# Four more chunks transposed by transfers instead of TensorE, in a retention layer followed by a Mish feed-forward

## The chip, the cores and the metric

The kernel runs on one core of one Trainium2 chip. A core has five engines that run their own instruction streams and meet at semaphores: TensorE (PE in the profile; its weight loads are listed as PEld), VectorE (DVE), ScalarE (ACT), GpSimd (POOL) and SyncE (SP). SP and POOL also issue the transfers (DMAs), which 16 DMA engines carry out. The metric is the time of one execution on the device, in microseconds, median of several runs. Before the change it is 296.61 us (three runs, 296.42 to 296.66).

## The reference

The inputs are q, k and v of shape (8 batches, 8 heads, 576 positions, 64), and two matrices, `w_in` (512 x 2048) and `w_out` (2048 x 512). The first part is causal attention without a softmax, with a decay per head; the second is a feed-forward layer with Mish on 4608 tokens of width 512.

```python
scores = scale * np.matmul(q, k.transpose(0, 1, 3, 2))
gamma = 1.0 - 2.0 ** (-5.0 - np.arange(H, dtype=np.float32))
Dmat = np.where(rel >= 0, gamma[:, None, None] ** rel[None, :, :], 0.0)   # rel = query - key position
attn = np.matmul(scores * Dmat, v)
x = attn.transpose(0, 2, 1, 3).reshape(B * S, H * D)
h = x @ w_in
g = h * np.tanh(softplus(h))
out = g @ w_out
```

## The kernel before

The decay is split into a factor on q, one on k and one on v by position, so that the attention becomes a linear recurrence: each batch is cut into chunks of 128 positions (four whole ones and a last one of 64, two such halves sharing one chunk), there are products inside a chunk, and a state of 64 x 64 per head is carried from chunk to chunk. In total there are 36 chunks. Chunks 0 to 7 are the first ones of the eight batches and are worked off by separate code at the start. From chunk 8 (`N0`) on every chunk goes through the same steps:

- `load(n)` (L298): three transfers issued by POOL bring q, k and v as float32. `vraw` has seven buffers, q and k (`qkraw`) have five. `paced` (L292) makes each load of chunks 12 and 13 wait until the sixth load before it has landed.
- `step_p(n)`, called P (L322): two VectorE instructions multiply q and k with their factors and write `qks` in bf16 (four buffers).
- `step_v(n)`, called V (L333): one instruction scales v into `vs`; on VectorE for n under 20, on POOL after that.
- `step_t(n)`, called T (L342): q and k are needed with the head dimension on the partitions. For n under `NT` (14) TensorE transposes `qks` in eight pieces (L351) into a PSUM bank, and ScalarE copies them to `qkT` (in two halves for chunks 8 to 11, L354 and L355, the second of which is put off by `flush`; in one copy for 12 and 13, L357). From chunk 14 on SP issues one transposing transfer from `qks` to `qkT` (L359). SP issues these in order with the stores of the output.
- `states` (L409) multiplies k with v for two chunks, and `sum_up` (L444) adds the products to the running state on VectorE (`total`, L452 to L464); a cast to `ssb` (L467) follows later.
- `step_s` (L364) forms the scores inside two chunks from `qkT`, `step_m` (L377) masks them on VectorE (`sm`).
- `visit(n)` (L524) belongs to chunks n and n + 1: it puts the state products of the next two chunks, the output products of these two (from `sm`, `vs`, `ssb` and `qkT`) and the scores of the next two on TensorE, and copies the result to `xT`, the input of the feed-forward part.
- `hold(n)` (L520) lets POOL copy one element of `qkT` of chunk n. As POOL works in order, its later loads are not issued until the transfer of that chunk has landed.

The feed-forward part works on tiles of four chunks. `g1(t, f)` makes one of 16 slices of the hidden layer of tile t (four matmuls of 128 x 512, then Mish on ScalarE), `g2(t, i)` a quarter of the 16 matmuls of a row block of the output. `product` (L551) issues one such matmul; while the counter `halved` is over 0, a matmul that is neither the first nor the last of its sum is issued as two of half the width.

The order of all work is written out by hand and fixed for each engine. The change lies in the loop over `u` from 0 to 23 (L753): its first 16 steps make the hidden layer of tile 1, the last 8 the first half of its output. Between them, dictionaries say at which `u` the steps of chunks 8 to 15 are put in (`ps` for P, `vs` for V, `ts_` for T). The visit of chunks 8 and 9 is at `u` = 17, that of 10 and 11 at `u` = 22; the states of chunks 8 and 9 are formed at `u` = 10, their cast to `ssb` is at `u` = 13. Loads of chunks 12, 13, 14, 15 and 16 are issued at `u` = 4, 8, 12, 16 and 20. The loop behind it (L800), over tiles 2 and up, is the same before and after.

Of the kernel before, what the change touches and what calls it, by code (L numbers as in the profile page):

```python
# [9 lines left out]
F32 = mybir.dt.float32  # L10
BF16 = mybir.dt.bfloat16
# [5 lines left out]
def kernel(  # L17
# [18 lines left out]
    nc = tc.nc  # L36
    B, H, S, D = q.shape
# [9 lines left out]
    NT = 14  # L47
# [242 lines left out]
    issued = []  # L290

    def paced(ins, n):  # L292

        if N0 + 3 < n < N0 + 6:
            behind(ins, issued[-6])
        issued.append(ins)

    def load(n, gate=None):  # L298
# [4 lines left out]
        vr = io.tile([P, H, D], F32, name="vraw", bufs=7)  # L303
        live[n] = {"qkr": qkr, "v": vr}
        for t, src in ((qkr[:, 0], q), (qkr[:, 1], k), (vr, v)):
            if c < 4:
                ins = nc.gpsimd.dma_start(  # L307
                    out=t, in_=src[b, :, ds(P * c, P), :].rearrange("h p d -> p h d"))
                paced(ins, n)
# [12 lines left out]
    def step_p(n):  # L322
        c = chunks[n][1]
        qks = io.tile([P, 2, H, D], BF16, name="qks", bufs=4)
        live[n]["qks"] = qks
        slots = qks.rearrange("p i (g x y) d -> p (i g) y x d", x=2, y=2)
        heads = live[n]["qkr"].rearrange("p i (g y x) d -> p (i g) y x d", x=2, y=2)
        factors = gqk[:, c].rearrange("p i (g y x) -> p (i g) y x", x=2, y=2)
        for y in range(2):
            nc.vector.tensor_tensor(slots[:, :, y], heads[:, :, y],  # L330
                                    factors[:, :, y].unsqueeze(3).to_broadcast([P, NP, 2, D]), op=OP.mult)
# [10 lines left out]
    def step_t(n, gate=None):  # L342
        flat = live[n]["qks"].rearrange("p i h d -> p (i h d)")
        qk = tr.tile([P, 2, NP, P], BF16, name="qkT", bufs=6)
        if n < NT:
            if n in (N0 + 2, N0 + 4):
                tp = ps_st.tile([P, 2 * NP, P], BF16, name="st")
            else:
                tp = ps_sc.tile([P, 4 * NP, P], BF16, name="sc")[:, 0:2 * NP]
            for i in range(2 * NP):  # L350
                nc.tensor.transpose(tp[:, i, :], flat[:, ts(i, P)], ident)  # L351
            if n < N0 + NCH:

                nc.scalar.copy(qk[:, 0], tp[:, 0:NP])  # L354
                later.append(lambda: nc.scalar.copy(qk[:, 1], tp[:, NP:2 * NP]))  # L355
            else:
                nc.scalar.copy(qk.rearrange("p i n t -> p (i n) t"), tp)  # L357
# [392 lines left out]
    ps = {0: 0, 4: 1, 8: 2, 11: 3, 18: 5, 21: 6, 23: 7}  # L750
    vs = {0: 0, 5: 1, 9: 2, 13: 3, 18: 4, 19: 5}
    ts_ = {3: 0, 7: 1, 12: 2, 14: 3, 19: 4, 21: 5}
    for u in range(24):  # L753
        j, w = divmod(u, 4)
        halved[0] = 2 if 0 < u < 5 else 0
        if u in ps:
            att(N0 + ps[u], "P")
        if u == 11:
            step_m(N0)
        if u in vs:  # L760
            att(N0 + vs[u], "V")
# [13 lines left out]
        elif u == 16:  # L775
            att(N0 + 4, "P")
# [3 lines left out]
        elif u == 22:  # L780
            visit(N0 + 2, ((ps_h, "hp"), (ps_h, "hp")), (act, dve))
            att(N0 + 6, "T")
# [6 lines left out]
        if u in ts_:  # L789
            att(N0 + ts_[u], "T")  # L790
# [107 lines left out]
```

## Time and profile before

| What | Value |
|---|---|
| Time, median of 3 runs | 296.61 us (296.42 to 296.66) |
| Profiled execution | 297.28 us, of which the span is 295.6 us |
| TensorE busy | 286.1 us, 97% of the span |
| VectorE, ScalarE, GpSimd busy | 140.0, 128.1, 124.9 us |
| Granted TensorE clock | 1.0 over the whole span |
| Transposing transfers | 22, median 2.8 us from issue to landing |
| Transposes of chunks by TensorE (L351) | 48 instructions, six chunks |
| Data moved by DMA | 47.45 MB, mean 161 GB/s |

Times in the views are counted from the start of the span. A line of a timeline gives the start, the duration, the engine, the line of the kernel, the operation, what it writes and reads, and how often; in square brackets it gives the idle time of the engine before it and what ended that. Matmuls overlap in their pipeline: one of 128 x 512 is listed with 0.38 us, but one starts every 0.216 us. A line of the windows gives, after the length of the window, the busy time and number of instructions of PE, PEld, DVE, ACT and POOL, then the granted clock, the share of the 16 DMA engines' time that packets took, and GB/s. Packets that take turns on an engine can add up to a share of over 1. A line of waits gives total us, how often, and the longest. In the DMA view q0 is the queue of the transfers that POOL issues and q1 that of SP; a line gives packets, MB and the share of the 16 engines' time. The loop over `u` begins at 48 us; the visit of chunks 8 and 9 begins at 65.8, that of 10 and 11 at 72.7; the loop over tiles 2 and up begins at 75.6.

### The profile page before, as it was taken

What the parts mean: (1) busy time and instruction counts of PE and PEld (TensorE: products, weight loads), DVE (VectorE), ACT (ScalarE), POOL (GpSimd) and SP (SyncE); (2) the same over time, 40 slices, a digit from 0 to 9 for tenths busy, and PEclk for the clock granted to TensorE, in tenths of its full rate; (3) what the DMA queues carried; (4) which work ended last, traced back from release to release, by engine and by line L of the source; (5) the groups of instructions that cost most, each with busy time, mean ns of one, the idle gap of its engine ahead of it and who ended that gap; (6) DMA issues with size and microseconds to landing.
All of it is one profiled execution on the core that took longest, in us unless ns stands there. A gap on an engine that the chain in (4) does not pass through costs nothing.

```text
span 295.6 us, 7898 instructions
## 1 busy us (share of the span) xinstructions
PE 286.1 (97%) x3447; PEld 159.7 (54%) x3486; DVE 140.0 (47%) x252; ACT 128.1 (43%) x210; POOL 124.9 (42%) x163
## 2 busy tenths in 40 slices
PE   7899999999999999999999999999999999999995
PEld 4666887556567454447645454545454544444443
DVE  5861549399954829454655454535453221000011
ACT  3856226776545534443443434343435333333200
POOL 8944678880167195855483636392020000000000
PEclk9999999999999999999999999999999999999999
DMA  7999999982498889799476837374222111011121
GB/s 154 234 204 204 205 328 337 336 237 85 109 270 190 168 229 254 232 145 330 116 204 164 260 90 237 108 229 115 68 71 71 38 38 65 9 35 49 59 71 71
DMA packets 44067, 47.45 MB, mean 161 GB/s; under 512 B 25984, under 2 KB 33152, under 8 KB 44032
## 3 DMA queue, kind: packets, MB, share of 16 engines
q0 software_dynamic: 15120, 31.20, 41.6%
q1 hardware_dynamic: 28768, 15.54, 20.7%
q8 instruction: 27, 0.44, 0.6%
q10 hardware_dynamic: 144, 0.20, 0.2%
q14 instruction: 8, 0.07, 0.1%
HBM read 37.75 MB, written 9.44 MB: 160 GB/s over the span
## 4 chain that ended last, share of the span: by engine, by line
PE 93%; DMA 2%; issue 1%; ACT 1%; POOL 1%; DVE 0%; POOLq 0%
PE hp L553 41%; PE ops L553 30%; PE hp L558 6%; PE ops L558 4%; DMA gT<-in_q_dram 2%; PE sc L373 1%; PE sc L428 1%; PE hp L504 1%; PE hp L487 1%; PE hp L634 1%; PE st L558 1%; POOL gT L107 1%; PE st L428 1%; PE sc L351 1%; PE sc L200 1%
## 5 line engine op out<-in xcount | busy, mean ns | idle before, releaser
L553 PE MATMUL hp<-xT,w_in_t 128*128 128x512 bf16 (+1 forms) x505 | 125.9, 376 | 0.9
L590 ACT ACTIVATE gT<-hp 128x512 bf16<-128x512 f32 x142 | 84.8, 598 | 95.3 <-PE hp L553 88.8
L553 PE MATMUL ops<-w_out_t,gT 128*128 128x512 bf16 x403 | 99.9, 379 | 2.0 <-issue 1.9
L553 PEld LDWEIGHTS <-w_in_t 128*128 128x128 bf16 x527 | 51.4, 98 | 53.9 <-issue 0.4
L553 PEld LDWEIGHTS <-gT 128*128 128x128 bf16 x470 | 44.7, 98 | 51.3
L642 DVE COPY res<-ops 128x512 f32<-128x512 f32 x28 | 19.3, 690 | 85.3 <-PE ops L553 85.2
L330 DVE TENSOR_TENSOR qks<-qkraw,gqk 128x512 bf16<-128x512 f32 x56 | 36.9, 709 | 0.0
L307 POOL DMA_DIRECT2D qkraw<-in_q_dram x24 | 21.5, 898 | 23.5 <-ACT gT L590 15.0
L337 POOL TENSOR_TENSOR vs<-vraw,gv 128x512 bf16<-128x512 f32 x16 | 16.8, 1068 | 25.0 <-PE hp L487 25.0
L516 DVE CAST xT<-hp 128x512 bf16<-128x512 f32 x13 | 9.0, 691 | 30.8 <-PE hp L504 30.8
L307 POOL DMA_DIRECT2D vraw<-in_v_dram x24 | 21.8, 907 | 1.8 <-DMA vraw<-in_v_dram 1.0
L307 POOL DMA_DIRECT2D qkraw<-in_k_dram x24 | 21.3, 886 | 1.0 <-DMA vpair<-in_v_dram 0.7
L516 ACT CAST xT<-hp 128x512 bf16<-128x512 f32 x14 | 8.2, 586 | 28.5 <-PE hp L504 28.5
L558 PEld LDWEIGHTS <-gT 128*128 128x128 bf16 x180 | 17.3, 98 | 3.7
L464 DVE TENSOR_TENSOR total<-sc,total 128x256 f32<-128x256 f32 x40 | 16.9, 422 | 1.0
L379 DVE TENSOR_TENSOR sm<-sc,mask 128x1024 bf16<-128x1024 f32 x14 | 17.0, 1214 | 0.6 <-PE sc L373 0.6
L558 PE MATMUL hp<-xT,w_in_t 128*128 128x256 bf16 x104 | 15.9, 272 | 0.0
L558 PEld LDWEIGHTS <-w_in_t 128*128 128x128 bf16 x106 | 10.4, 98 | 6.6 <-issue 0.2
L522 POOL COPY held<-qkT 128x1 bf16<-128x1 bf16 x8 | 1.5, 189 | 27.8 <-DMA qkT<-qks 27.8
L467 ACT CAST ssb<-total 128x768 bf16<-128x768 f32 (+3 forms) x13 | 11.6, 895 | 3.2 <-DVE total L464 3.2
L558 PE MATMUL ops<-w_out_t,gT 128*128 128x256 bf16 x96 | 12.4, 273 | 0.2
L553 PE MATMUL hp<-w_out_t,gT 128*128 128x512 bf16 x49 | 12.0, 379 | 0.2 <-issue 0.2
(132 smaller groups left out, 243.3 us busy)
## 6 DMA issues: line engine op xcount, KB each, us to landing
out_dram<-res SPq DMA_DIRECT2D x31, 256.0 KB, 2.4
qkraw<-in_q_dram POOLq DMA_DIRECT2D x24, 256.0 KB, 4.4
qkraw<-in_k_dram POOLq DMA_DIRECT2D x24, 256.0 KB, 4.5
vraw<-in_v_dram POOLq DMA_DIRECT2D x24, 256.0 KB, 4.7
w_out_t<-in_moe_w_out_dram POOLq DMA_DIRECT2D x4, 512.0 KB, 12.3
gT<-in_k_dram POOLq DMA_DIRECT2D x8, 128.0 KB, 7.1
gT<-in_v_dram POOLq DMA_DIRECT2D x2, 512.0 KB, 6.6
w_in_t<-in_moe_w_in_dram POOLq DMA_DIRECT2D x2, 512.0 KB, 10.3
```

Of the source, the lines that this page charges most:

```text
L307: ins = nc.gpsimd.dma_start(out=t, in_=src[b, :, ds(P * c, P), :].rearrange("h p d -> p h d"))
L330: nc.vector.tensor_tensor(slots[:, :, y], heads[:, :, y], factors[:, :, y].unsqueeze(3).to_broadcast([P, NP, 2, D]), op=OP.mult)
L337: engine.tensor_tensor(vs, live[n]["v"], gv[:, c, :].unsqueeze(2).to_broadcast([P, H, D]), op=OP.mult)
L379: nc.vector.tensor_tensor(sm.rearrange("p e x n i -> p (e x n) i"), live[n]["sc"].rearrange("p e x n i -> p (e x n) i"), mask.unsqueeze(1) ...
L428: ins = nc.tensor.matmul(to, lhsT=ks, rhs=vs, start=(x is not None or j == 0 and p == 0), stop=True, skip_group_check=True)
L464: nc.vector.tensor_tensor(new[:, k], st[:, j, x], total[b], op=OP.add)
L467: casts.append(lambda copy: copy(lows[:, 0:k], new[:, 0:k]))
L516: copy(xts[t][:, :, ds(P * s, 2 * P)].rearrange("p h (x j i) -> p j h x i", x=2, j=2)[:, j], both[j])
L553: newest[0] = nc.tensor.matmul(to, lhsT=w, rhs=x, start=first, stop=last)
L558: nc.tensor.matmul(to[:, ts(j, n)], lhsT=w, rhs=x[:, ts(j, n)], start=False, stop=False, skip_group_check=True)
L590: done = nc.scalar.activation(gts[t][:, f, :], hp, AX.Mish)
L642: copy(ot, ops)
```

## The change

Chunks 10 to 13 are no longer transposed by TensorE and copied by ScalarE: `NT` falls from 14 to 10, so SP issues four more transposing transfers, at `u` = 8, 9, 10 and 11 for chunks 10, 11, 12 and 13, and the one of chunk 14 moves to `u` = 18. On VectorE, P of 11 and 12 and V of 11 come before the sums of the states (`u` = 9), P of 13 follows those sums, P of 14 comes at `u` = 14. `paced` is gone. At `u` = 13 POOL holds for chunk 13's transfer, so the loads of chunk 15 and up are issued after it has landed. `qks` gets a fifth buffer, `vraw` loses its seventh. `halved` splits 29 more products, in `u` = 12 to 21; with the 32 transposes gone, the number of TensorE's instructions, weight loads among them, falls by six only.

```diff
-    NT = 14
+    NT = 10
...
-    issued = []
-    def paced(ins, n):
-        if N0 + 3 < n < N0 + 6:
-            behind(ins, issued[-6])
-        issued.append(ins)
...
-        vr = io.tile([P, H, D], F32, name="vraw", bufs=7)
+        vr = io.tile([P, H, D], F32, name="vraw", bufs=6)
...
-                paced(ins, n)
...
-        qks = io.tile([P, 2, H, D], BF16, name="qks", bufs=4)
+        qks = io.tile([P, 2, H, D], BF16, name="qks", bufs=5)
...
-            if n in (N0 + 2, N0 + 4):
-                tp = ps_st.tile([P, 2 * NP, P], BF16, name="st")
-            else:
-                tp = ps_sc.tile([P, 4 * NP, P], BF16, name="sc")[:, 0:2 * NP]
+            tp = ps_sc.tile([P, 4 * NP, P], BF16, name="sc")[:, 0:2 * NP]
...
-            if n < N0 + NCH:
-                nc.scalar.copy(qk[:, 0], tp[:, 0:NP])
-                later.append(lambda: nc.scalar.copy(qk[:, 1], tp[:, NP:2 * NP]))
-            else:
-                nc.scalar.copy(qk.rearrange("p i n t -> p (i n) t"), tp)
+            nc.scalar.copy(qk[:, 0], tp[:, 0:NP])
+            later.append(lambda: nc.scalar.copy(qk[:, 1], tp[:, NP:2 * NP]))
...
-    ps = {0: 0, 4: 1, 8: 2, 11: 3, 18: 5, 21: 6, 23: 7}
-    vs = {0: 0, 5: 1, 9: 2, 13: 3, 18: 4, 19: 5}
-    ts_ = {3: 0, 7: 1, 12: 2, 14: 3, 19: 4, 21: 5}
+    ps = {0: (0,), 4: (1,), 8: (2,), 11: (5,), 14: (6,), 23: (7,)}
+    vs = {0: (0,), 5: (1,), 18: (4,), 19: (5,)}
+    ts_ = {3: (0,), 7: (1,), 8: (2,), 9: (3,), 10: (4,), 11: (5,), 18: (6,)}
...
-        halved[0] = 2 if 0 < u < 5 else 0
-        if u in ps:
-            att(N0 + ps[u], "P")
+        halved[0] = 2 if 0 < u < 5 or 11 < u < 16 else 4 if 15 < u < 22 else 0
+        if u == 9:
+            att(N0 + 2, "V")
+            att(N0 + 3, "PV")
+            att(N0 + 4, "P")
+        for n in ps.get(u, ()):
+            att(N0 + n, "P")
...
-        elif u == 16:
-            att(N0 + 4, "P")
...
-            att(N0 + 6, "T")
...
+        for n in ts_.get(u, ()):
+            step_t(N0 + n)
+        if u == 13:
+            hold(N0 + 5)
```

6 lines of the change are left out of this document (2 added, 4 removed).

## The prediction

> **What bounds the kernel now.** I read the page's busy times first, then who waited for whom, then the timelines of TensorE (PE), VectorE (DVE) and GpSimd (POOL) around the edit, then the windows and the DMA view of the same stretch.
>
> ```profile
> PE 286.1 (97%) x3447; PEld 159.7 (54%) x3486; DVE 140.0 (47%) x252; ACT 128.1 (43%) x210; POOL 124.9 (42%) x163
> PE 93%; DMA 2%; issue 1%; ACT 1%; POOL 1%; DVE 0%; POOLq 0%
> ```
> ```profile
> PE ops L553 <- issue: 1.9, 12, 0.2
> ...
> PEld L351 <- DVE qks L330: 0.5, 1, 0.5
> ```
> PE is busy for 97% of the span and is 93% of the chain that ended last; its longest single wait inside the loops is 0.5 us. So what leaves PE's instruction stream comes off the time, unless a new wait of PE takes its place.
>
> TensorE, timeline (start, us, what):
> ```profile
> 60.51 0.61 PE L351 MATMUL st<-ident,qks 128*128 128x128 bf16 x8
> 60.95 0.38 PE L553 MATMUL hp<-xT,w_in_t 128*128 128x512 bf16 x1
> ...
> 66.21 0.20 PE L504 MATMUL ops<-qkT,ssb 64*64 64x64 bf16 x2
> ...
> 66.34 0.45 PE L373 MATMUL sc<-qkT 64*64 64x64 bf16 x32
> ...
> 71.27 0.62 PE L351 MATMUL sc<-ident,qks 128*128 128x128 bf16 x8
> 71.72 0.38 PE L553 MATMUL ops<-w_out_t,gT 128*128 128x512 bf16 x1
> ```
> The eight transposes of chunk 10 hold PE from 60.51 to 60.95. At 66.21 the visit of chunks 8 and 9 reads `ssb`, at 66.34 it reads `qkT` of chunks 10 and 11: these are the deadlines.
>
> VectorE, timeline:
> ```profile
> 53.24 0.68 DVE L337 TENSOR_TENSOR vs<-vraw,gv 128x512 bf16<-128x512 f32 x1
> 58.90 0.42 DVE L452 COPY total<-st 128x256 f32<-128x256 f32 x1 [4.98 <-PE st L428]
> 59.36 1.80 DVE L464 TENSOR_TENSOR total<-sc,total 128x256 f32<-128x256 f32 x4
> 61.08 1.28 DVE L330 TENSOR_TENSOR qks<-qkraw,gqk 128x512 bf16<-128x512 f32 x2
> 62.28 1.22 DVE L379 TENSOR_TENSOR sm<-sc,mask 128x1024 bf16<-128x1024 f32 x1
> 63.41 0.68 DVE L337 TENSOR_TENSOR vs<-vraw,gv 128x512 bf16<-128x512 f32 x1
> 64.01 1.05 DVE L467 CAST ssb<-total 128x1280 bf16<-128x1280 f32 x1
> ```
> DVE idles 4.98 us up to 58.90, then runs without a gap to `ssb` at 65.06. That is the only slack the edit can use, and the only place where it can hurt soon.
>
> POOL's issues of the k loads of chunks 12 and 13; windows (DMA share and GB/s at the end); landing of all transposing transfers; packets of both queues from 49 to 50 us:
> ```profile
> 50.06 0.88 POOL L307 DMA_DIRECT2D qkraw<-in_k_dram  x1 [0.25 <-issue]
> ...
> 52.69 0.89 POOL L307 DMA_DIRECT2D qkraw<-in_k_dram  x1
> ```
> ```profile
> 56.00:58.00 2.00, 2.00 (x14) 0.75 (x14) 0.00 (x0) 1.69 (x4) 2.00 (x4) 1.00 1.03 338
> ...
> 74.00:76.00 2.00, 1.89 (x9) 0.88 (x9) 1.91 (x3) 0.72 (x2) 0.00 (x0) 1.00 0.58 131
> ...
> 131.00:133.00 2.00, 2.00 (x11) 0.88 (x10) 0.67 (x2) 1.00 (x3) 1.75 (x2) 1.00 0.19 11
> ```
> ```profile
> DMA to landing us min/median/max: 2.7/2.8/5.5
> ```
> ```profile
> q1 hardware_dynamic: 169, 0.32, 82.7%
> q0 software_dynamic: 22, 0.06, 19.5%
> ```
> The DMA engines are full at 56 to 58 us (share 1.03), just where the new transposes go. One transpose alone costs them 0.58 x 2 = 1.16 us (74 to 76). From 131 to 133 a transpose was in flight, yet almost nothing moved (11 GB/s): a transpose can also get stuck.
>
> **The change part by part.**
>
> *PE loses 32 transposes.* By the start-to-start times of rows like the first above: chunk 10 0.44 us, chunk 11 (62.68 to 63.12) 0.44, chunk 12 (68.91 to 69.35) 0.44, chunk 13 0.45. Chunk 13's also began late: the four matmuls at 70.22 take 4 x 0.216 and end at 71.08, the transposes start at 71.27, for that wait on `qks`; so 0.19 more. Sum -1.96 us.
>
> *PE gains 29 split products* (8 in u = 12 to 15; 3, 4, 4, 3, 3, 4 in u = 16 to 21). Eight halves take 0.87 us in the chain of waits (37.70) where four whole ones take 0.86: at most 0.01 per four, 0.07 in all; at least nothing. I take +0.07.
>
> *ScalarE loses six copies* (4 x 0.58, 1.01, 1.03: 4.4 us). It is 43% busy and waits for PE; worth nothing. The PSUM banks they used are one user fewer; nothing waited for them.
>
> *VectorE.* Scaling of 11 (1.28), v of 11 (0.68), scaling of 12 (1.28) move ahead of `total`: 3.2 us into the idle 4.98, from 53.9. That needs q and k of 12: k was issued at 50.06 and landed 6.2 later, 56.26. So scaling 12 ends at 57.5, 1.4 before `total` can start. Scaling of 13 takes the place of that of 11 at 61.08; its k landed at 52.69 + 6.4 = 59.1. v of 11 no longer stands between `sm` and `ssb`: `ssb` then ends at 64.46. PE reaches L504 at 66.21 - 2 x 0.44 = 65.33. Slack 0.87 us. Scaling of 14, 1.28, follows `ssb`; its next reader is far.
>
> *Four transposes on SP,* ahead of the store of row block 1 and of all later ones. 10's `qks` is ready at 53.3, 11's at 55.2; both go out behind the last stores of tile 0. At 2.8 to 5.5 us from issue to landing they are there by 58 to 61; PE wants them at 66.34 - 0.88 = 65.46. 12's goes out at about 58 to 60, 13's after 62.4; due 73.21 - 1.77 = 71.4 at chunk 12's and 13's own products: covered.
>
> *What the transposes do to the loads.* Those of 10 and 11 take 2 x 1.16 = 2.3 us of full DMA engines; the loads behind them slip as much. 12's k then lands at 58.6, its scaling ends at 59.9, `total` starts 1.0 late, `ssb` ends at 65.46: PE waits 0.13. 13's k lands at 61.4: 0.3 late for its scaling, less than that 1.0. Lower bound: no slip (loads not held up), wait 0. Upper bound without sticking: a third transpose ahead of 13's k as well, 62.6 instead of 61.08, wait 1.5 - 0.87 = 0.65. I take +0.3, between 0.13 and the upper bound, since two lie ahead of 12's k for certain and the third starts about then.
>
> *Pacing of 12's and 13's loads goes.* Their issue comes some 1.2 us sooner (the wait shown for POOL at 48.93 is 1.2). The engines are full, so landing hardly moves: 0; at best it gives back part of the slip.
>
> *POOL holds until 13's transpose lands,* then chunk 15's loads. Landing 62.4 + 2.8 to 5.5 = 65 to 68; 15's q and k follow 0.9 apart and land 4.4 later, 70.5 to 73.3, where scaling 15 (75.83 - 1.9) wants them at 73.9; 16's three follow, k at 73 to 76, wanted at 76.9. POOL has no other work queued there. 0; cover left 0.6 us in the worst case.
>
> *Buffers* (`qks` 5, `vraw` 6): the sixth last v was scaled long before each load. 0.
>
> Sum against the profiled execution (297.28 us: span 295.6 and 1.68 around it): -1.96 + 0.07 + 0.3 = -1.59, 295.7. That execution was 0.67 above the median, so 295.0 on the median's scale.
>
> **The rivals.**
>
> *Turns.* The transposing queue gets one 256-byte packet for each load packet. From 55 to 63 us the load queue moved 706 packets; a transpose alone had 1039 in the second from 75 to 76. So 10's would stand at about two thirds when the loads run dry at 63.3, and end 0.4 later; 11's 1.16 later; landing takes 0.5: 65.4 to 65.8 against 65.46, a wait of PE of 0 to 0.35 at L373, and no slip of the loads. Time 294.7 to 295.1. Against it: from 49 to 50 us queue q1 moved 169 packets beside 22, so it isn't always turn by turn. The Trainium skill, DMA: Bandwidth & Descriptors, section Queues, rings and completion order, says that each DMA engine goes round its rings packet by packet; by that rule this rival would be the forecast, while the 169 to 22 of this trace disagree with it.
>
> *DVE late by a little more.* One of 10's and 11's transposes runs at half its solo speed, another 1.2 us on 12's k: `total` 2.2 late, PE waits 1.3; with a second one slow, 2.5. Time 296.0 to 297.2: no change that can be told.
>
> *A transpose sticks; slower.* Place: 10's or 11's transpose among the loads of 12 and 13. Price: the 2 us of 131 to 133 on top of 1.16 each, and the same for 12's before 13's k: k at 59.1 + 3 x 1.16 + 2.2 = 64.8. `ssb` ends 3.4 after scaling 13 starts, 68.2; PE waits 2.9; time 297.6. It decides from the point where 13's k lands later than 61.95 + 1.89 = 63.8 (or 12's later than 60.3). For it: transposes with loads about took 4.6 to 5.5 us, those in the quiet second half 2.7 to 2.8. Against it: one stuck transpose mostly shows where loads are few; under full load no transpose runs in this trace.
>
> *Chunk 15's loads come too late* behind the hold. Past the 0.6 of cover left, each us is hidden again by DVE's lead over the next visit; it would take two more. At most 295.5.
>
> **How the numbers follow.** Less than 0.2% (0.6 us) is about what a measurement of this kernel can't tell from no change. Forecast 0.40, turns 0.15, chunk 15 late 0.05: faster, 0.60. A little more late: half of 0.24, 0.12, ends within 0.2%, and the other 0.12 joins the stuck case (0.16): slower, 0.28. The range reaches from 294.4 (no wait at all, 294.7, and 0.3 for waits of 0.16 that vanish after the visits) to 297.6, the stuck case; above lie several stuck at once. The faster cases alone: 294.5 to 295.7.
>
> **What would show it.** L351's transposes fall from 48 to 16 and the transposing transfers grow from 22 to 26, with all 16 DMA engines full to some 66 us. Right: PE goes from the state products to the visit with a wait of under 0.7, and later loops keep their lengths. If PE waits on `ssb` or `sm` from VectorE there, and VectorE before that on a load, the slip was larger than 2.3; if PE waits on `qkT`, it was turns. The prediction is wrong if a transpose of 10 to 12 takes over 6 us to land, or if PE waits later than the second visit.

## The result and the profile after

The changed kernel takes 300.46 us in the median of six executions (298.97 to 301.45), the kernel before on the same chip 296.51 us (six executions, 296.09 to 296.89). The ratio is 1.0132 (95% interval 1.0103 to 1.0160): slower by 1.3%, 3.95 us. The prediction was 295.0 us, faster, with a range up to 297.6 us; sign and range were both wrong. The profiled execution of the changed kernel took 298.97 us (span 297.2), the shortest of its six.

Several of the kernels below scatter more than the kernel before: the runs of e2, e5 and e13 lie between 295.5 and 302.1 us, so for these the range is given beside the median. Executions over 1.5% above the shortest of the same kernel (two of e2, four of e5, two of e13, one of e8) are in the medians but not in the ratios.

The page of the changed kernel, busy times and the chain that ended last, and the queues of the transfers (packets, MB, share of the 16 engines' time):

```profile
PE 289.3 (97%) x3483; PEld 161.6 (54%) x3483; DVE 139.9 (47%) x252; ACT 124.4 (42%) x204; POOL 124.7 (42%) x164
PE 96%; issue 1%; ACT 1%; DVE 0%
q1 hardware_dynamic: 32992, 16.59, 24.1%
q8 instruction: 27, 0.44, 0.7%
```

TensorE is still the bound. It has 32 transposes fewer, and yet its busy time is longer by 3.2 us. That alone tells little: the records of before lack a few matmuls, and in the profile after some matmuls run at a lower clock.

TensorE, longest waits (us in total, how often, longest), then its timeline around the first visit:

```profile
PE sc L357 <- issue: 2.9, 1, 2.9
PE ops L170 <- DVE pos L135: 1.3, 1, 1.3
```
```profile
65.01 0.20 PE L488 MATMUL hp<-qkT,ssb 64*64 64x64 bf16 x2
65.03 0.31 PE L357 MATMUL sc<-qkT 64*64 64x64 bf16 x15
68.24 0.47 PE L357 MATMUL sc<-qkT 64*64 64x64 bf16 x17 [2.90 <-issue]
...
69.29 3.42 PE L542 MATMUL hp<-w_out_t,gT 128*128 128x256 bf16 x22
```

L488 reads `ssb` (L504 of before) and is not held up. L357 forms the scores of chunks 10 and 11 (L373 of before), 16 products for each. TensorE stands still for 2.90 us, and the place of the stop says what it lacked. The stop lies behind the 15th product, ahead of the last one of chunk 10. The transfer of chunk 10 had landed at 63.02, and this product waits for no semaphore; the wait for `qkT` of chunk 11 is on the weight load of the 17th product. So TensorE stood without instructions, which is what the profile's "issue" leaves room for. Queue q8 on the page brings the instructions, in 27 packets of 16 KB. One of these was fetched from 65.55 to 66.68, and the restart at 68.24 follows 1.56 us later. The transposing transfer of chunk 11 landed at 68.12, 0.12 us before the restart. So had the instructions been there, TensorE would have waited at the 17th product almost as long: two delays lie one over the other here.

That these packets are blocks of 256 instructions of TensorE follows from where it stops. In ten of the kernels of this document there are sixteen stops of 0.3 to 5.8 us that end 1.3 to 1.6 us after a packet of q8. The number of weight loads ahead of the stop, each followed by one matmul, is 735, 991, 1375, 2399 or 2783 every time. These numbers differ by multiples of 128 loads, which are 256 instructions, and the packet that ended before the restart is by this count the right one, the 5th, 7th, 10th, 18th or 21st. In the changed kernel the stop is behind load 735. TensorE began the block before that at 58.11, and the 5th packet was fetched only 7.4 us later; in before it was 1.6 us (58.55 and 60.10).

Behind the wait 22 half-width products take 3.42 us, 0.155 each, where eight took 0.87 before, 0.109 each.

VectorE, the same stretch:

```profile
55.84 1.29 DVE L321 TENSOR_TENSOR qks<-qkraw,gqk 128x512 bf16<-128x512 f32 x2 [0.78 <-DMA qkraw<-in_k_dram]
58.45 0.43 DVE L436 COPY total<-st 128x256 f32<-128x256 f32 x1 [1.32 <-PE st L412]
60.63 1.28 DVE L321 TENSOR_TENSOR qks<-qkraw,gqk 128x512 bf16<-128x512 f32 x2
62.97 0.81 DVE L451 CAST ssb<-total 128x1280 bf16<-128x1280 f32 x1
66.72 1.29 DVE L321 TENSOR_TENSOR qks<-qkraw,gqk 128x512 bf16<-128x512 f32 x2 [2.94 <-DMA qkraw<-in_k_dram]
```

The scaling of chunk 12 and that of chunk 13 are in time, `ssb` is ready at 63.78. Only the scaling of chunk 14 (66.72) waits for its load, and TensorE doesn't need that one until much later.

GpSimd's hold, and the windows from 56 us on:

```profile
70.00 0.19 POOL L506 COPY held<-qkT 128x1 bf16<-128x1 bf16 x1 [11.75 <-DMA qkT<-qks]
```
```profile
56.00:58.00 2.00, 2.00 (x71) 1.03 (x69) 1.13 (x2) 1.85 (x4) 1.80 (x3) 1.00 1.17 288
58.00:60.00 2.00, 1.96 (x29) 1.01 (x25) 1.44 (x4) 0.60 (x2) 0.25 (x1) 1.00 1.32 112
60.00:62.00 2.00, 2.00 (x15) 1.27 (x13) 1.97 (x5) 1.20 (x3) 0.00 (x0) 1.00 1.16 153
62.00:64.00 2.00, 2.00 (x16) 1.39 (x15) 1.78 (x2) 1.45 (x3) 0.00 (x0) 1.00 1.20 139
...
66.00:68.00 2.00, 0.00 (x0) 0.00 (x0) 1.28 (x2) 0.00 (x0) 0.00 (x0) 0.91 0.98 93
68.00:70.00 2.00, 1.76 (x69) 1.51 (x70) 1.26 (x3) 0.77 (x2) 0.00 (x1) 0.50 0.84 186
70.00:72.00 2.00, 2.00 (x15) 1.59 (x14) 1.93 (x6) 0.31 (x1) 1.66 (x3) 0.73 0.99 131
72.00:74.00 2.00, 2.00 (x19) 1.61 (x17) 1.08 (x2) 1.04 (x2) 2.00 (x3) 1.00 0.80 193
```

The last three columns are the granted clock, the DMA share and GB/s. From 58 to 64 us the packets take as much of the engines' time as before the change (share 1.16 to 1.32) or more, but move 112 to 153 GB/s. In the window of before at 56 to 58 us a share of 1.03 moved 338. Part of this is that transposes move fewer bytes in the same time: the prediction's 1.16 us for the 256 KB of one make 226 GB/s. But even at that rate the 0.81 MB moved from 58 to 64 us would take 3.6 us of the engines, and their packets took 7.4. After the wait the granted clock is 0.50 and then 0.73.

The transposing transfers of chunks 10 to 14 (the median of all 26 of the execution is 2.8):

```profile
DMA to landing us min/median/max: 3.4/10.3/13.6
```

One by one, from the records of issue and landing: chunk 10 at 52.74 to 63.02 (10.3 us), 11 at 54.49 to 68.12 (13.6), 12 at 58.18 to 68.98 (10.8), 13 at 62.28 to 69.86 (7.6), 14 at 69.11 to 72.53 (3.4). The prediction had 2.8 to 5.5 us for each.

### The profile page after: what moved, and what is told of

It reads as the page before. It is cut to its first block, busy times and chain, and to the rows that moved or that the text cites. A ratio compares the mean times of both kernels' runs of the same rounds, so it can differ in the third digit from the quotient of the medians.

```text
span 297.2 us, 7938 instructions
## 1 busy us (share of the span) xinstructions
PE 289.3 (97%) x3483; PEld 161.6 (54%) x3483; DVE 139.9 (47%) x252; ACT 124.4 (42%) x204; POOL 124.7 (42%) x164
## 4 chain that ended last, share of the span: by engine, by line
PE 96%; issue 1%; ACT 1%; DVE 0%
PE hp L537 40%; PE ops L537 30%; PE hp L542 8%; PE ops L542 4%; PE sc L357 2%; PE sc L412 1%; PE hp L488 1%; PE ops L170 1%; PE hp L471 1%; PE hp L618 1%; PE st L542 1%; PE st L412 1%; PE sc L200 1%; PE sc L222 1%; PE ops L173 1%
## 5 line engine op out<-in xcount | busy, mean ns | idle before, releaser
L537 PE MATMUL ops<-w_out_t,gT 128*128 128x512 bf16 x409 | 101.0, 379 | 0.0
L537 PEld LDWEIGHTS <-w_in_t 128*128 128x128 bf16 x519 | 50.6, 98 | 52.7 <-issue 0.4
L537 PEld LDWEIGHTS <-gT 128*128 128x128 bf16 x449 | 42.9, 98 | 49.1
L542 PEld LDWEIGHTS <-gT 128*128 128x128 bf16 x222 | 21.8, 100 | 5.0
L542 PE MATMUL hp<-xT,w_in_t 128*128 128x256 bf16 x120 | 18.3, 273 | 0.0
L542 PEld LDWEIGHTS <-w_in_t 128*128 128x128 bf16 x122 | 11.9, 98 | 7.7 <-issue 0.2
L542 PE MATMUL ops<-w_out_t,gT 128*128 128x256 bf16 x110 | 14.1, 273 | 0.0
L542 PE MATMUL hp<-w_out_t,gT 128*128 128x256 bf16 x84 | 11.5, 287 | 0.0
## 6 DMA issues: line engine op xcount, KB each, us to landing
w_in_t<-in_moe_w_in_dram POOLq DMA_DIRECT2D x2, 512.0 KB, 10.3
```

Of the source, the lines that this page charges most:

```text
L537: newest[0] = nc.tensor.matmul(to, lhsT=w, rhs=x, start=first, stop=last)
L542: nc.tensor.matmul(to[:, ts(j, n)], lhsT=w, rhs=x[:, ts(j, n)], start=False, stop=False, skip_group_check=True)
```

## The experiments

Each kernel was timed beside the kernel before on the same chip. The letters in the quoted expectations number the theories as they stood when each was written; the text below names the mechanisms. A diff is against the changed kernel unless it says otherwise.

### e1 and e5: chunks 10 and 11 back on TensorE

e1 is one line: chunks 10 and 11 are transposed by TensorE, at the early places (`u` = 8 and 9).

```diff
-    NT = 10
+    NT = 12
```

> Chunks 10 and 11 are transposed by TensorE again (NT = 12, at u = 8 and 9); 12 and 13 stay with the transfers; all else as in the changed kernel. Theory A (transposing transfers and loads jam each other while both are in flight, and only the transfer of chunk 11 is due before the jam ends): the transfers of 12 and 13 still take 5 to 11 us, but land before 71 us, TensorE never waits over 0.5 us, the granted clock is 1.0 throughout, and the time is 296.5 - 0.44 - 0.64 + 0.07 = 295.5. Rival D (the new order on VectorE and POOL is what costs): TensorE still waits at the visit of chunks 8 and 9 and the time is 298 or more.

Measured: 298.65 us (298.35 to 299.13), ratio 1.0069 (1.0046 to 1.0091). The wait at the first visit's scores is gone and so is the low clock (1.000 over the span). But two other waits are there:

```profile
PE hp L537 <- DVE qks L321: 1.5, 1, 1.5
PE sc L357 <- ACT qkT L341: 1.2, 1, 1.2
```

The 1.2 us, at 58.75, are for ScalarE's copies, which come later than TensorE needs them. The 1.5 us, from 75.65 to 77.16, are put down to VectorE's scaling, but the product that ends them reads `xT`, whose casts had ended by 74.65. It stands behind weight load 991, and a block had been fetched until 75.75, 1.41 us before. So this is a wait for instructions and not for the scaling of chunk 11, as which the expectation of e5 counts it. So e1 settled less than it should: it brought waits of its own. e5 puts both back to their old places and, for chunk 10, to its old bank:

```diff
-    NT = 10
+    NT = 12
...
+            if n == N0 + 2:
+                tp = ps_st.tile([P, 2 * NP, P], BF16, name="st")
...
-    ts_ = {3: (0,), 7: (1,), 8: (2,), 9: (3,), 10: (4,), 11: (5,), 18: (6,)}
+    ts_ = {3: (0,), 7: (1,), 10: (4,), 11: (5,), 12: (2,), 14: (3,), 18: (6,)}
```

> Chunks 10 and 11 are transposed by TensorE at u = 12 and 14, the places that they had before the change (chunk 10's in the bank that it had there); 12 and 13 by transfers at u = 10 and 11, as in the changed kernel. In the run with them at u = 8 and 9 TensorE waited 1.5 us for the scaling of 11 and 1.2 us for ScalarE's copies. Theory A (only a transfer that is due before the jam ends costs time): those two waits go, the transfers of 12 and 13 land by 67 us against 71, no other wait appears, and the time is 296.4 - 0.44 - 0.64 + 0.07 = 295.4 (295.1 to 296.0). Rival D (the rest of the change costs as well): 296.5 or more.

Measured: 300.81 us, in two groups, 297.05 to 297.76 and 300.56 to 302.05; ratio 1.0072 (1.0037 to 1.0106). The transfers of 12 and 13 landed in 5.7 and 2.8 us and nothing waited for them. The profiled execution, one of the long ones, stood still in the middle of a row of products whose data had long been there:

```profile
74.33 0.38 PE L540 MATMUL hp<-xT,w_in_t 128*128 128x512 bf16 x1
78.88 1.70 PE L540 MATMUL hp<-xT,w_in_t 128*128 128x512 bf16 x5 [4.17 <-issue]
```

This stop is behind weight load 991, again at the edge of a block. One block was fetched from 67.10 on, the next only from 76.55 to 77.49, 1.39 us before the restart, while chunk 14's transposing transfer (66.91 to 75.07, 8.2 us) and the loads of chunks 15 and 16 were in flight. The prediction had no such mechanism; e4, e7, e9, e10 and e14 bear on it too.

### e2 and e6: loads kept away from the transposes

e2 lets chunk 14's loads wait for 11's transfer, and puts chunk 14's scaling and transfer back to the places of before:

```diff
-    ps = {0: (0,), 4: (1,), 8: (2,), 11: (5,), 14: (6,), 23: (7,)}
+    ps = {0: (0,), 4: (1,), 8: (2,), 11: (5,), 21: (6,), 23: (7,)}
...
+        if u == 11:
+            hold(N0 + 3)
...
```

> The changed kernel with chunk 14's loads behind chunk 11's transfer (a hold at u = 11), and so chunk 14's scaling at u = 21 and its transfer after the second visit, where they were before. Theory A (loads beside the transposing transfers make the jam): the loads of 12 and 13 end by 60 us, chunk 11's transfer lands by 64, TensorE doesn't wait for it, and the time is 294.7 to 295.5. Rival C (several transposing transfers in flight jam each other, loads or not): chunk 11's transfer lands after 66 as in the changed kernel, TensorE waits over 2 us and the time is 299 or more.

Measured: 298.80 us (296.51 to 301.38), ratio 1.0057 (1.0027 to 1.0087). In the profiled execution 11's transfer took 9.1 us and landed at 65.34, and L357 began at 65.56 without a wait. Beside the loads of 12 and 13 alone the transfers of 10, 11 and 12 still took 10.0, 9.1 and 7.0 us. What TensorE lost in that execution lies behind the second visit: 1.1 us for `gT` at 79.2 and 0.8 for `vs` at 83.1. The median is between the two forecasts of the time.

e6 holds back 13's loads as well; the scaling and the transfer of 13, and those of 14, move behind them:

```diff
-            if j < 5:
+            if j == 2:
+                pass
+            elif j < 5:
                 load(N0 + j + 3)
...
+        if u == 10:
+            hold(N0 + 3)
+            load(N0 + 5)
...
```

> The changed kernel with the loads of chunks 13 and 14 behind chunk 11's transfer; scaling of 13 at u = 14, its transfer at u = 15 with the hold behind it, scaling of 14 at u = 21 and its transfer after the second visit. When the transfers of 10 and 11 are on their way only chunk 12's loads are left beside them. Theory A: 10's and 11's transfers land by 59 and 61 us (under 7 us each), the DMA engines move over 250 GB/s between 56 and 60 us, TensorE doesn't wait at the first visit; a wait may come at the second, for 13's transfer, due at 71. Time 294.7 without one, up to 298 with one. Rival C (transposing transfers jam each other): 11's lands after 65 again.

Measured: 299.72 us (299.19 to 301.13), ratio 1.0100 (1.0082 to 1.0118). With two chunks' loads fewer beside them, the transfers of 10, 11 and 12 took 4.8, 4.0 and 4.4 us. Together with e4 below, where one transfer alone among the loads is slow, this shows that it is the loads in flight that make them slow. The price comes elsewhere. 13's transfer is now late, and SP is still busy issuing it (65.63 to 68.16) when TensorE needs a mark from SP that stands behind it in SP's queue (`written`, an empty instruction on SP between the two halves of the visit's products):

```profile
68.27 0.26 PE L488 MATMUL hp<-qkT,ssb 64*64 64x64 bf16 x2 [2.84 <-SPq L388]
```

And the loads held back meet the next transfers: those of 14, 15 and 16 took 10.5, 9.0 and 9.8 us.

### e3: the wait filled with idle work

13 matmuls of 128 x 512 on zeros are put ahead of the scores of chunks 10 and 11. They compute nothing that is used.

```diff
+        if n == N0 + 2:
+            idle = sc.rearrange("p e x n i -> p (e x n i)")
+            for _ in range(13):
+                nc.tensor.matmul(idle[:, 0:512], lhsT=zeros[:, 0:P], rhs=zeros, start=True, stop=True,
+                                 skip_group_check=True)
```

> The changed kernel with 13 idle matmuls of 128 x 512 (13 x 0.216 = 2.8 us) ahead of the scores of chunks 10 and 11, into a bank that the scores overwrite; TensorE is busy while the transfer of chunk 11 is under way. Theory (the stall costs twice: once as a wait, once as a lower clock behind it): the granted clock stays at 1.0 in 66 to 72 us, the wait left is under 1 us, and the time is 1 to 2 us below the changed kernel's, 298.5 to 299.5. Rival (the lower clock comes from something else, or costs nothing): clock and time as in the changed kernel, 300.5, or more if the transfer lands later.

Measured: 298.62 us (298.03 to 299.50), ratio 1.0070 (1.0043 to 1.0096): more work, and 1.84 us less than the changed kernel's 300.46. The transfer of 11 was no faster (14.8 us, landed 69.18).

```profile
67.83 0.22 PE L362 MATMUL sc<-qkT 64*64 64x64 bf16 x2
69.30 0.44 PE L362 MATMUL sc<-qkT 64*64 64x64 bf16 x30 [1.24 <-issue]
70.08 2.57 PE L547 MATMUL hp<-w_out_t,gT 128*128 128x256 bf16 x22
```

The stop is now behind the second product, 13 products sooner, as many as idle matmuls were put ahead: its place moves with the instructions and not with chunk 11's data. The block had been fetched until 67.79, 1.50 us before the restart. The 22 half-width products take 2.57 us where they took 3.42 in the changed kernel, and one starts every 0.109 us, so the clock was not lowered. (The trace of this execution holds no record of the clock, so that a granted clock of 1.00 says nothing here.) So the low clock comes from the wait and not from the transfers. By the medians its price is 1.84 us.

### e4 and e8: a single transfer, and the pacing back

e4 leaves only chunk 11 to a transfer; 10, 12 and 13 are transposed by TensorE, and GpSimd's hold is on 11.

```diff
-        if n < NT:
+        if n < NT or n in (N0 + 2, N0 + 4, N0 + 5):
...
-    ts_ = {3: (0,), 7: (1,), 8: (2,), 9: (3,), 10: (4,), 11: (5,), 18: (6,)}
+    ts_ = {3: (0,), 7: (1,), 8: (2,), 9: (3,), 12: (4,), 14: (5,), 18: (6,)}
...
-            hold(N0 + 5)
+            hold(N0 + 3)
```

> Of chunks 10 to 13 only chunk 11 is transposed by a transfer; 10, 12 and 13 are transposed by TensorE (12 and 13 at u = 12 and 14), and POOL holds for chunk 11's. Loads as in the changed kernel. Theory A (loads jam it): this one transfer, alone in its kind, takes 8 us or more from issue to landing. Rival C (transposing transfers jam each other): it takes at most 5.5 us, as those with loads about took before the change. Time under A 297 to 299, if it lands after 65.5; under C 296.1.

Measured: 304.30 us (304.05 and 304.55), ratio 1.0258 (1.0232 to 1.0285), the slowest of all. The one transfer of 11 took 8.2 us among the loads: it needs no second transpose to be slow. What made the kernel so slow is again the instruction block, behind weight load 991:

```profile
79.86 3.17 PE L537 MATMUL ops<-w_out_t,gT 128*128 128x512 bf16 x7 [5.76 <-issue]
```
```profile
74.00:76.00 2.00, 0.10 (x12) 0.10 (x1) 1.75 (x3) 0.59 (x1) 0.00 (x0) 1.00 1.18 110
76.00:78.00 2.00, 0.00 (x0) 0.00 (x0) 1.97 (x5) 0.00 (x0) 0.00 (x0) 0.54 0.50 174
78.00:80.00 2.00, 0.14 (x1) 0.13 (x2) 1.93 (x5) 0.00 (x0) 0.00 (x0) 0.50 0.71 131
```

One block's packet at 69.14 took 2.4 us (the others of this execution take 0.9 to 1.5). The next one began at 77.46, within 0.03 us of the landing of chunk 14's stuck transpose (67.90 to 77.49), and ended at 78.49, 1.37 us before the restart.

e8 puts the removed `paced` back into the changed kernel.

```diff
+    issued = []
+
+    def paced(ins, n):
+
+        if N0 + 3 < n < N0 + 6:
+            behind(ins, issued[-6])
+        issued.append(ins)
...
+                paced(ins, n)
```

> The changed kernel with the pacing of the loads of 12 and 13 put back. Theory A (pacing spreads these loads by 1 us only, the jam is made by loads that are in flight all the same): chunk 11's transfer still lands after 66 us and the time stays at 299 to 302. Rival E (it was the missing pacing that let loads run into the transfers): 11's lands by 65 and the time falls to 296 or less.

Measured: 302.15 us (299.47 and 304.84), no ratio with an interval from two executions so far apart. 11's transfer landed at 72.95, after 18.6 us. The missing pacing is not what makes the transposes slow. In this profile the two delays stand one behind the other. The block was fetched until 70.45, the 16th product follows 1.51 us later, and only then comes a wait that bears the mark of chunk 11's `qkT`:

```profile
66.52 0.29 PE L366 MATMUL sc<-qkT 64*64 64x64 bf16 x15
71.97 0.26 PE L366 MATMUL sc<-qkT 64*64 64x64 bf16 x1 [5.15 <-issue]
73.00 0.43 PE L366 MATMUL sc<-qkT 64*64 64x64 bf16 x16 [0.77 <-DMA qkT<-qks]
```

### e7, e9 and e10: everything but the transfers, and the split products

e7 is the kernel before, with VectorE's order, the buffers, the loads without pacing and the 29 splits of the changed kernel, but with all transposes on TensorE at their old places. Against before:

```diff
-                paced(ins, n)
...
-        halved[0] = 2 if 0 < u < 5 else 0
+        halved[0] = 2 if 0 < u < 5 or 11 < u < 16 else 4 if 15 < u < 22 else 0
+        if u == 9:
+            att(N0 + 2, "V")
+            att(N0 + 3, "PV")
+            att(N0 + 4, "P")
...
```

> The kernel before with all of the change but the transfers and the hold: VectorE's new order, no pacing, five buffers of qks and six of vraw, the 29 split products; chunks 10 to 13 transposed by TensorE at their old places. Theory A (the transfers alone cost): 296.4 + 0.07 - 0.19 (the wait for the scaling of 13 goes) = 296.3, within 0.3 of the kernel before. Rival D (the new order or the missing pacing costs): over 297.5.

Measured: 299.23 us (298.34 to 300.81), ratio 1.0096 (1.0067 to 1.0124). That was a surprise: no early transpose at all, and 2.8 us lost. The waits have no late data in them; two of TensorE's three gaps are in runs of equal products:

```profile
PE hp L503 <- issue: 1.3, 2, 0.7
PE hp L552 <- issue: 1.0, 1, 1.0
```

The instruction count suggested the cause: the page has 3515 weight loads for 3486, so with as many matmuls 58 instructions more. (The expectations count 6956 instructions for the kernel before, the page makes 2 x 3486 = 6972; the differences between the kernels are the same.) e9 is e7 without the 29 splits, e10 is before with nothing but them.

```diff
-        halved[0] = 2 if 0 < u < 5 or 11 < u < 16 else 4 if 15 < u < 22 else 0
+        halved[0] = 2 if 0 < u < 5 else 0
```

> The kernel of the run e7 (before, with VectorE's work moved, the pacing of the loads gone and the buffers changed; all eight transposes of chunks 8 to 13 on TensorE at their old places) without the 29 further split products, so that TensorE has as many instructions as before, 6956. Theory B (what cost e7 its 2.7 us is the place of TensorE's instructions in the blocks in which they are fetched, since its idle times had no late data and before has none there): about 296.5 us, 295.9 to 297.2, and the idle times of 0.8, 0.9 and 1.4 us at the state products and the product by halves are gone. Rival: VectorE's order, the buffers or the loads without pacing cost it: again 298.3 to 299.5, with idle times of TensorE for data.

> Before with only the 29 further split products (58 instructions more on TensorE, no work more): Theory B: the blocks of TensorE's instructions end elsewhere from 80 us on, as in e7: 298 to 299.5 us, with idle times of 0.7 to 1.4 us that no data explains. Rival (the split products cost only their own small price, 29 times 2 to 3 ns): 296.5 to 296.9 us.

Measured: e9 296.39 us (295.94 to 297.28), ratio 0.9993 (0.9981 to 1.0006). e10 299.08 us (298.11 to 300.11), ratio 1.0077 (1.0056 to 1.0098). Both fall where the place of the blocks puts them. VectorE's new order, the missing pacing and the buffers cost nothing together, and 58 instructions that do no further work cost 2.6 us. In e10's profile four stops at the edges of blocks, 1.45, 0.70, 0.44 and 0.34 us, add up to 2.9. The first, TensorE, timeline:

```profile
72.78 0.26 PE L504 MATMUL hp<-qkT,ssb 64*64 64x64 bf16 x9
74.49 0.25 PE L504 MATMUL hp<-qkT,ssb 64*64 64x64 bf16 x7 [1.45 <-issue]
74.68 1.04 PE L553 MATMUL ops<-w_out_t,gT 128*128 128x512 bf16 x4
```

It stops in the middle of 16 products that read the same finished data. A block was fetched from 72.03 to 73.16, 1.33 us before the restart. The same distance stands at the other gaps of this kind: 1.45 us at e10's second one (fetched by 96.52, restart at 97.97), 1.42 in e7 (72.73, 74.15). In before, the fetch nearest to this place is at 73.72 to 74.69, and the waits show no gap there. The gaps lie at the visits or just behind them. There TensorE uses up its instructions fastest: in before's windows 151 matmuls and 151 weight loads from 70 to 75 us, against 29 and 28 from 75 to 80.

### e11 and e14: half the change, and the number of instructions restored

e11 is e5 with chunk 14's scaling and transfer as late as before, and with 16 splits in place of 29, so that TensorE has as many instructions as before (3486 weight loads on the page). Against e5:

```diff
-    ps = {0: (0,), 4: (1,), 8: (2,), 11: (5,), 14: (6,), 23: (7,)}
+    ps = {0: (0,), 4: (1,), 8: (2,), 11: (5,), 21: (6,), 23: (7,)}
...
-        halved[0] = 2 if 0 < u < 5 or 11 < u < 16 else 4 if 15 < u < 22 else 0
+        halved[0] = 2 if 0 < u < 5 else 2 if u == 18 else 4 if 18 < u < 23 else 0
...
+            step_t(N0 + 6)
...
```

> Chunks 10 and 11 transposed on TensorE at their old places, 12 and 13 by transfers, the transfer of 14 after the second visit as before, chunk 14's work on VectorE as before; the splits are chosen so that TensorE has 6956 instructions as before, and the products behind the second visit begin at the same place in the stream. Theory A and B together (the jam costs where a transpose falls due at once or holds back an instruction block; the place of the blocks costs the rest): 16 transposes fewer are worth 16 times 55 ns, 0.9 us, nothing waits for the transfers of 12 and 13, and no block comes late: 295.3 to 296.0 us, faster than before. Rival (transposing transfers among the loads cost by themselves, wherever their result is due): 297 us or more, with waits of TensorE for its instructions or lower clock between 60 and 80 us.

Measured: 295.51 us (295.04 to 295.64), ratio 0.9963 (0.9950 to 0.9975): faster than both kernels. The transfers of 12 and 13 were issued at 57.51 and 61.43, took 6.8 and 3.6 us, and are due at the second visit's scores at 71.18. All its waits on the page of waits are those of the start:

```profile
PE ops L170 <- DVE pos L135: 1.3, 1, 1.3
PE sc L222 <- DVE sm L226: 0.5, 1, 0.5
```

The gain also checks the prediction's price of a transpose: chunks 12 and 13 gave 0.44 + 0.45 + 0.19 = 1.08 us there, less 16/29 of 0.07 for the splits, 1.04. Measured are 296.51 - 295.51 = 1.00.

e14 takes e11's two edits against e5 apart: it has the 29 splits again (26 instructions more than before) and keeps chunk 14's transfer late. Against e11:

```diff
-        halved[0] = 2 if 0 < u < 5 else 2 if u == 18 else 4 if 18 < u < 23 else 0
+        halved[0] = 2 if 0 < u < 5 or 11 < u < 16 else 4 if 15 < u < 22 else 0
```

> The kernel of e11 with the changed kernel's 29 splits in place of its 16, 6982 instructions on TensorE, the transfer of 14 after the second visit as in e11. Theory B (the place of the blocks): 297 to 299.5 us, with idle times of TensorE of 0.7 to 2 us that no data explains. Rival (in e5 it was the early transfer of 14 among the loads of 15 and 16 alone): 295.3 to 296.2 us, as e11.

Measured: 296.40 us (295.85 to 298.01), ratio 1.0003 (0.9985 to 1.0020), between the two expectations. The place of the blocks costs 0.9 us here (a gap of 0.93 from start to start at 74.19, 1.54 us after a fetch ended). e5 has the same instructions on TensorE and takes 297.05 to 297.76 us in five executions and 300.56 to 302.05 in seven. So moving chunk 14's scaling and transfer ahead, among the loads of 15 and 16, costs another 1 to 5 us.

### e12 and e13: the two causes in the changed kernel

e12 is the changed kernel with three more splits, as many instructions as before; e13 does the same to e2.

```diff
-        halved[0] = 2 if 0 < u < 5 or 11 < u < 16 else 4 if 15 < u < 22 else 0
+        halved[0] = 2 if 0 < u < 5 or 11 < u < 16 else 4 if 15 < u < 22 else 3 if u == 22 else 0
```

> The changed kernel with 3 more split products, so that TensorE has 6956 instructions as before. Theory A (the jam of transposes and loads is what costs in the changed kernel; its profile shows no wait for an instruction block): no better than 299 to 301 us, the scores of chunks 10 and 11 wait 2 to 5 us at the first visit, the granted clock falls behind it. Rival B (the place of the instruction blocks costs most of it): 295.5 to 297.5 us.

> The kernel of e2 (chunk 14's loads held behind 11's transfer, chunk 14's work on VectorE and its transfer as late as before) with 3 more split products, 6956 instructions on TensorE as before. If the jam at the first visit and the place of the blocks are all that costs: 294.8 to 296.2 us, faster than before by up to the 1.96 us of the 32 transposes. Rival (transfers beside loads cost TensorE in further ways, by late products of ScalarE and VectorE among other things): 297 to 299.5 us, as e2.

Measured: e12 300.20 us (299.10 to 302.09), ratio 1.0124 (1.0093 to 1.0155), the same as the changed kernel. Its profile has the wait at L357 again, and 11's transfer landed at 69.02 after 13.5 us:

```profile
69.30 0.34 PE L357 MATMUL sc<-qkT 64*64 64x64 bf16 x17 [3.59 <-issue]
```

So the total number is not what the changed kernel pays for. But the three splits are at `u` = 22, behind the first visit, and leave the edge of the block there where it was: the stop is again behind the 15th product, and 1.47 us after a fetch that ended at 67.83. The late block and the late transfer end within 0.3 us of each other again, so this run does not tell them apart, and the expectation is wrong that the changed kernel's profile has no wait for a block.

e13 took 298.81 us (295.54 to 301.79), ratio 1.0041 (1.0015 to 1.0067). That is the rival's range. Its shortest execution, 295.54, is below every one of the kernel before, but most are far above: the first visit is in time (11's transfer landed at 62.72), but chunk 14's loads now lie later and push chunk 15's into the next transposes. Those of 14 and 15 took 10.1 and 8.0 us, the load of 15's k came late, and the third visit, that of chunks 12 and 13, pays. VectorE and TensorE:

```profile
81.33 1.29 DVE L321 TENSOR_TENSOR qks<-qkraw,gqk 128x512 bf16<-128x512 f32 x2 [4.69 <-DMA qkraw<-in_k_dram]
```
```profile
83.88 0.22 PE L412 MATMUL sc<-vs,qks 64*64 64x64 bf16 x2 [2.44 <-DVE vs L328]
```

## Why the prediction was wrong

**The step that failed** is the one on SP's transfers: "At 2.8 to 5.5 us from issue to landing they are there by 58 to 61". They took 10.3 and 13.6 us and were there at 63.0 and 68.1, the second 2.7 us later than the 65.46 at which TensorE was to want it. The durations came from transfers that ran where loads were few, and no row of the trace of before had a transpose under full load. The prediction said so, and still took the quiet range for the sum. The nearest rows it had against it were the 4.6 to 5.5 us with loads about. With one chunk's loads beside them (e6) that size is right, 4.0 to 4.8; with those of 12 and 13 it is 7 to 10 (e2) or 6 to 8 (e13), with those of 14 too 10 to 14.

**What TensorE waited for.** The prediction had no term for TensorE's instructions. By its place, behind the 15th of 32 products, the wait of 2.90 us was for the next block of them, and chunk 11's transfer landed 0.12 us before its end. Both delays have the same ground: where transposes met the loads of three chunks, the 5th block was fetched 7.4 us (changed kernel), 8.1 (e12), 8.7 (e3) and 11.3 (e8) after TensorE began the one before, in before 1.6, in e6 1.0 and in e13 2.7. So the failed step gives the size of the wait, but not all of what it was for. In between lie e2 and e4 with fewer loads or fewer transposes, 4.7 and 4.8. Whether it is more than chance that block and transfer end within 0.3 us of each other in three of these executions (1.0 in e8) no run shows.

**The step "What the transposes do to the loads"** treated the DMA engines as a fixed amount of work, 1.16 us for each transpose, with the loads slipping by the sum, +0.3 us. The direction was wrong for the loads that mattered: chunk 12's k was there by 55.84 and 13's by 60.63, and `ssb` was ready sooner than forecast (63.78 for 64.46). It was the transposes that were late. And the amount is not fixed: in the windows from 58 to 64 us the same share of the engines' time moved less than half the bytes.

**The clock** was in no term of the sum. After the wait it was 0.50 and 0.73 in two windows of 2 us, which takes about 0.5 x 1.76 + 0.27 x 2.00 = 1.4 us from the products in them; e3 puts it at 1.8 in the median. The Trainium skill, TensorE: Matmul & The Clock Gate, section What's actually happening, says that the array runs at half its clock after an idle window of about 3.4 us and at the full clock after as long a busy one. The 0.50 agrees with it, and so does the return to 1.00 by 72 us. Here a gap of 3.1 us from start to start was enough; gaps of 1.9 us in e1 and 1.7 in e10 left the clock at 1.00. In e13 the wait of 2.44 us at the third visit was followed by a low clock too (0.993 over its span), so an idle time well below the page's window was enough there.

**The sum redone** for the two profiled executions: -1.96 + 0.07 for TensorE's instructions; +2.9 for the wait; +1.4 for the clock: +2.4. The changed kernel's execution was already 0.7 ahead in the code that both share, at weight load 352 (38.29 for 38.96), which leaves +1.7, against 298.97 - 297.28 = 1.69 measured. The median of the changed kernel lies 1.5 above its profiled execution. That execution was its shortest; e12, whose time is near the median, waited 3.59 us.

**The 29 split products, +0.07.** Their own duration was right. But that a split has no price beyond its duration was wrong: alone they cost 2.6 us (e10), by the place at which blocks of instructions end. What they cost in the changed kernel, where 32 transposes go as they come, no run shows by itself. The Trainium skill, Runtime: NRT & Kernel Launch, section Instruction fetch mechanics, has blocks of 16 KiB, 256 instructions, and calls the cost of crossing one mostly hidden. The size agrees (27 packets, 0.44 MB, and stops a multiple of 256 instructions apart); that it is hidden does not hold here, in idle times of 0.3 to 1.5 us in e10 and of 2.9 to 5.8 us where a transpose was in flight (the changed kernel, e4, e5, e8, e12).

**Right:** TensorE's -1.96, by the half that e11 keeps, 1.00 for 1.04. VectorE's order, the pacing, the buffers at nothing (e9). ScalarE's copies and the hold at nothing, as far as no wait of TensorE in the profile comes from either; 13's transfer landed at 69.9, later than the 65 to 68 that the hold was worked out from.

**The rivals.** "Turns" had the data that came late, `qkT` for the scores, but priced the wait at 0 to 0.35 us. It still took the engines' speed as given and only shared it out. From 57 to 59 us queue q1 moved 465 packets and the loads' q0 93, so the transposes had more than half of them, and still came late. The rule of the Trainium skill, DMA: Bandwidth & Descriptors, section Queues, rings and completion order, that an engine goes round its rings packet by packet, gives the turns and not how long a packet takes, and the time went there. The page counts several descriptors as one packet, and no run shows whether a packet of the profile is one of these, so neither these counts nor the prediction's 169 to 22 can confirm or refute the rule. "A transpose sticks" had the sign, and by chance the very size of the wait, 2.9 us, but at `ssb` by late loads, which did not happen. Its chance, with that of its neighbour 0.28 for slower, was held down by rows of quiet stretches. The prediction's own test, a transpose of over 6 us, did catch it.

**Open.** Why transposes and loads slow each other within the DMA engines is not shown, only that they do and that fewer loads cure it. That the block of instructions waits behind the same jam rests on times: how late blocks are fetched in the kernels with and without it, and e14 against e5. No record links a block's fetch to a transfer. No run has only one of the two, late block or late transfer, at the first visit, so what each would cost alone is an estimate from when they ended. Nor does the trace show what happens in the 1.3 to 1.6 us between a block's arrival and the restart.

## What to carry to other kernels

A transposing transfer is cheap for TensorE only while its result has slack: price it by a row with the loads beside it that it will really meet, and where there is none, allow several times the quiet duration. Here each had 10 to 14 us from issue to due date: those of 12 and 13 in e11 met the end of the loads, took 3.6 and 6.8 us and gained 1.0 us; those of 10 and 11 met three chunks' loads, and with them the kernel lost 4. After a change in the number of instructions on the bounding engine, look for its waits on "issue" in runs of equal products. Count the instructions up to such a stop: if kernels that differ stop at the same count, or at counts a whole number of blocks apart, it is the fetch of the instructions. A landing close to the restart proves nothing; look which instruction bears the wait. A version with the old number of instructions helps only if the old number is reached ahead of the stop. Holding back a load to clear the way moves the collision to the next pair of transfers; follow it through the next visits.

## What the runs showed of the hardware

- A transposing transfer of one chunk (128 x 1024 in bf16, 256 KB) lands 2.7 to 2.8 us after issue alone, 4 to 5 beside one chunk's loads (e6), 6 to 10 beside those of two (e2, e13: chunks 10 to 12), 10 to 14 beside those of three (changed kernel: chunks 10 to 12), 18.6 in the worst case (e8). Issuing it then keeps SP for up to 5.6 us instead of 1.3 (7.7 in e8), with all that is queued there, marks between other engines included (2.84 us in e6).
- TensorE's instructions come in blocks of 256. It restarts 1.3 to 1.6 us after a late block was fetched (sixteen stops in ten kernels). The 5th block was fetched 7.4 to 11.3 us after TensorE began the one before where transposes met the loads of three chunks (changed kernel, e3, e8, e12), 1.0 to 2.7 in e6, e13 and before.
- 58 instructions more on TensorE, with no more work, cost 2.6 us (e10); restoring the number behind the stop gains nothing (e12).
- A wait of 3 us cost another 1.4 (profile of the changed kernel) to 1.8 us (medians, e3) in clock; 13 idle matmuls in the wait saved that.
